# A spectral filter and a feed-forward block on one core: the steps of batch 0 reordered, one threshold moved to VectorE, all of batch 1's first DFT placed in the feed-forward stage

## The chip, the cores and the metric

The kernel runs on one core of a Trainium2 chip. The core has five engines that work side by side and wait for one another through semaphores: TensorE (PE in the profile, its weight loads PEld), VectorE (DVE), ScalarE (ACT), GpSimd (POOL) and SyncE (SP), which here issues every transfer. The metric is the device time of one execution in microseconds (us); lower is better.

## The reference

The input is x, 8 batches of 3008 positions with 256 features. What is computed, shortened:

```python
X = np.fft.rfft(x, axis=1)                       # along the 3008 positions
Yr = Xr @ w_r - Xi @ w_i + b_r
Yi = Xr @ w_i + Xi @ w_r + b_i
Y  = sign(Y) * max(abs(Y) - 0.01, 0)             # both parts, soft threshold
y  = np.fft.irfft(Y, n=3008, axis=1)
h  = y.reshape(24064, 256) @ w_in                # 256 -> 2048
out = (h - tanh(h)) @ w_out                      # 2048 -> 256
```

w_in and w_out are float64 in memory.

## The kernel before

The transform of 3008 = 47 x 64 positions is done in two stages of matmuls each way. `Forward` is the first stage (47 points): a chunk holds 4 of the 32 groups of a batch, and each chunk has two *parts* (split a tile into a high and a low fp32r half, L210; three matmuls, L217 to L219; copy out of PSUM, L233) and one store to the scratch tensor `a`. `Spectrum` is everything between the two inner stages for a pair of frequencies, 12 pairs in a batch: load `at`, second DFT stage (`transform`, L266), products with the linear layer (`cross`, L354, into the PSUM tiles ps_v and ps_t), threshold, inverse stage (L373) and a store of `zo` to the scratch tensor `z`. `Chunk` is the feed-forward block (FFN) for 5 of the 256 groups, 470 columns: load `zin` from `z`, last inverse stage (`time`, L403), then for each of 16 blocks f of 128 hidden features `up` (six matmuls into h, L416; tanh on ScalarE, L419; g = h - tanh on VectorE, L421; gh, a cast on ScalarE, L423; gl on VectorE, L425) and `down` (six matmuls into o, L437). One *slot* is one up and one down; up runs two slots ahead of down.

The program has two stages. The first (from L484) is written out by hand, and each engine works in the order of the code: batch 0's Forward, batch 0's Spectrum (`WholeSpectrum`, in plain fp32), conversion of part of the float64 weights, and the first two chunks' load and time. In it the loop of L537 runs over i = 0 to 12 and in one turn does the transform of pair i, the products of pair i-1, the threshold of pair i-2 and the inverse of pair i-3. In the loop of this stage a threshold is four adds on VectorE (L311, 64x256 each, tb from SBUF and ps_v from PSUM), two Relu activations on ScalarE (L363 `up`, L365 `mn`), and a subtraction on VectorE (L369 `mn`, the *join*). `sum` (L343) is a VectorE add that the products of the next turn need. The products of a pair need its sum, its copy xf (L338 on ScalarE) and a free ps_v buffer (there are two: that of the pair two before, free when that pair's four adds are done). `common` (L358) is the ScalarE copy tb that the four adds read.

A conversion of a *unit* of 128x512 weights from float64 is four closures (`split_f64`, L155): exponent, mantissa, scale, parts. Together they are four TENSOR_SCALAR (L161, L162, L165, L166) and two SCALAR_TENSOR_TENSOR (L172, L175) on VectorE, three operations on ScalarE (L167, L168, L176) and two on GpSimd (L169, L177). There are 16 units; the first stage before loads 6 of them, and works their closures off from the list `ops`.

The second stage is the FFN, from L599: `put(slot, ...)` files what is to run in which slot, and a scheduler orders each engine's instructions within the dependencies. The first 32 slots take chunks 0 and 1 by turns, f = 0 to 15. Ten units, six of batch 1's eight Forward chunks and batch 1's Spectrum are filed there.

## Time and profile before

| what | value |
|---|---|
| time, median of 3 runs (lowest to highest) | 2720.56 us (2716.45 to 2723.26) |
| time of the profiled execution | 2719.45 us |
| its span, first to last instruction | 2717.2 us |
| PE busy, share of the span | 2682.9 us, 99% |
| VectorE busy | 1746.0 us, 64% |
| ScalarE busy | 1388.9 us, 51% |
| GpSimd busy | 48.9 us, 2% |

The profiled execution's time is its span and 2.25 us around it. A row of the timeline gives start, length, engine, line, operation, what it writes and reads, how many instructions the row merges, and in brackets the idle time of the engine before it with what ended it. Matmul lengths overlap: the next one starts before the one before has ended, so from a row's start to the next row's start is its real price.

### The profile page before, as it was taken

The numbers are of one execution on the slowest core, as the hardware profiler recorded it, in microseconds if no ns is written. First come the engines' busy times: TensorE is split into PE (matmuls) and PEld (weight loads), VectorE is DVE, ScalarE is ACT, GpSimd is POOL, SyncE is SP. The second block draws the span as 40 slices with busy tenths as digits, with TensorE's granted clock in tenths as the row PEclk, the third lists the DMA queues.
The fourth block names the chain that finished last, engine by engine and source line by source line (L and its number), as shares of the span: only waits on it lengthen the run. The fifth ranks groups of instructions, "written<-read, shape, count | busy, mean of one in ns | idle before, by whom it ended". The sixth has DMA issues, their size and how long they took to land.

```text
span 2717.2 us, 36997 instructions
## 1 busy us (share of the span) xinstructions
PE 2682.9 (99%) x14159; PEld 2390.0 (88%) x14159; DVE 1746.0 (64%) x3056; ACT 1388.9 (51%) x2606; POOL 48.9 (2%) x39
## 2 busy tenths in 40 slices
PE   8889999999999999999999999999999999999999
PEld 6679888999889998899988999899988999998989
DVE  5796775766656666567665666656675667655555
ACT  5664455444554445545455454645446544444445
POOL 1230000000000000000000000000000000000000
PEclk9899999999999999999999999999999999999999
DMA  6442114111141113211023110311104111100000
GB/s 198 146 127 65 47 52 125 42 49 36 36 115 49 38 36 96 75 46 49 28 58 101 38 53 30 105 58 48 49 23 123 46 42 40 35 22 22 20 19 17
DMA packets 105137, 163.49 MB, mean 60 GB/s; under 512 B 7488, under 2 KB 70976, under 8 KB 104864
## 3 DMA queue, kind: packets, MB, share of 16 engines
q1 hardware_dynamic: 104960, 161.13, 19.6%
q8 instruction: 111, 1.82, 0.3%
q14 instruction: 66, 0.54, 0.1%
HBM read 86.13 MB, written 74.97 MB: 59 GB/s over the span
## 4 chain that ended last, share of the span: by engine, by line
PE 92%; DVE 5%; ACT 2%; issue 1%; DMA 1%; POOL 0%; SPq 0%; DVEq 0%; ACTq 0%
PE o L437 36%; PE h L416 36%; PE ps_v L286 4%; PE ps_i L403 4%; PE ps_f L266 3%; PE ps_t L286 2%; DVE y L311 1%; PE ps_f L217 1%; PE ps_f L219 1%; PE ps_f L218 1%; PE ps_i L322 1%; PE ps_i L323 1%; PE ps_i L321 1%; DVE g L421 1%; DVE gl L425 0%
## 5 line engine op out<-in xcount | busy, mean ns | idle before, releaser
L421 DVE TENSOR_TENSOR g<-h,th 128x470 f32<-128x470 f32 (+1 forms) x832 | 532.0, 639 | 554.6 <-ACT th L419 547.0
L419 ACT ACTIVATE th<-h 128x470 f32<-128x470 f32 (+1 forms) x832 | 464.1, 558 | 765.9 <-PE h L416 765.6
L425 DVE TENSOR_TENSOR gl<-g,gh 128x470 fp32r<-128x470 f32 (+1 forms) x832 | 534.5, 643 | 289.3 <-ACT gh L423 204.8
L423 ACT CAST gh<-g 128x470 fp32r<-128x470 f32 (+1 forms) x832 | 483.1, 581 | 392.6 <-DVE g L421 384.3
L437 PE MATMUL o<-gh,wout_l 128*128 128x470 f32 (+1 forms) x1664 | 632.8, 380 | 0.1
L437 PE MATMUL o<-gl,wout_h 128*128 128x470 f32 (+1 forms) x1664 | 617.1, 371 | 3.1 <-DVE gl L425 3.1
L437 PE MATMUL o<-gh,wout_h 128*128 128x470 f32 (+1 forms) x1664 | 616.1, 370 | 0.0
L416 PE MATMUL h<-yh,win_l 128*128 128x470 f32 (+1 forms) x1664 | 481.0, 370 | 4.1 <-DVE g L421 4.1
L416 PE MATMUL h<-yl,win_h 128*128 128x470 f32 (+1 forms) x1664 | 481.1, 370 | 1.6 <-DVE yl L408 1.5
L416 PE MATMUL h<-yh,win_h 128*128 128x470 f32 (+1 forms) x1664 | 480.1, 369 | 0.0
L437 PEld LDWEIGHTS o<-gl,wout_h 128*128 128x128 f32 x1664 | 313.1, 188 | 44.8 <-DVE gl L425 6.2
L416 PEld LDWEIGHTS h<-yh,win_l 128*128 128x128 f32 x1664 | 310.6, 188 | 41.9 <-DVE g L421 5.1
L437 PEld LDWEIGHTS o<-gh,wout_l 128*128 128x128 f32 x1664 | 313.4, 188 | 35.2 <-DVE ot L446 1.3
L416 PEld LDWEIGHTS h<-yl,win_h 128*128 128x128 f32 x1664 | 310.7, 188 | 37.7 <-DVE yl L408 2.2
L437 PEld LDWEIGHTS o<-gh,wout_h 128*128 128x128 f32 x1664 | 313.9, 189 | 32.2
L416 PEld LDWEIGHTS h<-yh,win_h 128*128 128x128 f32 x1664 | 310.7, 188 | 35.6
L311 DVE TENSOR_TENSOR y<-tb,ps_v 64x256 f32<-64x256 f32 x384 | 160.0, 417 | 9.7 <-ACT tb L358 5.7
L403 PEld LDWEIGHTS ps_i<-i,zin 96*128 96x128 f32 x1024 | 126.2, 192 | 3.0
L403 PE MATMUL ps_i<-i,zin 96*128 96x94 f32 x1024 | 127.7, 272 | 0.0
L91 DVE TENSOR_TENSOR x_l<-xt,x_h 94x512 fp32r<-94x512 f32 x128 | 87.8, 694 | 54.1 <-ACT x_h L90 54.1
L266 PEld LDWEIGHTS ps_f<-f,at 128*128 128x128 f32 x768 | 99.5, 189 | 9.3 <-issue 4.3
L266 PE MATMUL ps_f<-f,at 128*128 128x128 f32 x768 | 101.1, 273 | 1.8 <-DMA at<-a 1.8
(96 smaller groups left out, 2131.6 us busy)
## 6 DMA issues: line engine op xcount, KB each, us to landing
xt<-in_x SPq DMA_DIRECT2D x64, 384.0 KB, 3.6
at<-a SPq DMA_DIRECT2D x96, 256.0 KB, 2.8
z<-zo SPq DMA_DIRECT2D x96, 256.0 KB, 2.0
out<-ot SPq DMA_DIRECT2D x50, 470.0 KB, 3.0
a<-st SPq DMA_DIRECT2D x56, 384.0 KB, 3.2
zin<-z SPq DMA_DIRECT2D x44, 480.0 KB, 4.3
w_raw<-in_moe_w_in SPq DMA_DIRECT2D x8, 512.0 KB, 4.2
w_raw<-in_moe_w_out SPq DMA_DIRECT2D x8, 512.0 KB, 4.4
```

Of the source, the lines that this page charges most:

```text
L91: rest.tensor_tensor(out=lo, in0=src, in1=hi.bitcast(F32), op=ALU.subtract)
L217: nc.tensor.matmul(pv, f1h, xl, start=True, stop=False)
L266: nc.tensor.matmul(pv[:, t, jj], self.at[:, jj, t * P:(t + 1) * P], rhs, start=True, stop=True)
L286: nc.tensor.matmul(dst, lhs[:, t], rhs[:, t, :], start=n == 0, stop=n == 5)
L311: nc.vector.tensor_tensor(out=y[ri * 64:(ri + 1) * 64, jj, :], in0=common(jj, ri), in1=self.vv[jj * 64:(jj + 1) * 64, ri * D:(ri + 1) * D] ...
L403: nc.tensor.matmul(ps[:, k * 94:(k + 1) * 94], self.zt[:, k, t * P:(t + 1) * P], i2t[:, p * 94:(p + 1) * 94], start=True, stop=True,)
L416: nc.tensor.matmul(h[:, :n], lhs[:, t, f * P:(f + 1) * P], rhs[:, t, :n], start=k == 0, stop=k == 5)
L419: nc.scalar.activation(out=th[:, :n], in_=h[:, :n], func=AF.Tanh)
L421: nc.vector.tensor_tensor(out=g[:, :n], in0=h[:, :n], in1=th[:, :n], op=ALU.subtract)
L423: nc.scalar.copy(out=gh[:, :n], in_=g[:, :n])
L425: nc.vector.tensor_tensor(out=gl[:, :n], in0=g[:, :n], in1=gh[:, :n].bitcast(F32), op=ALU.subtract)
L437: nc.tensor.matmul(self.o[t][:, :n], lhs[:, f, t * P:(t + 1) * P], rhs[:, :n], start=f == 0 and k == 0, stop=f == NF - 1 and k == 2,)
```

## The change

Seven things change. (1) In the loop, `sum` of pair i and the products of pair i-1 stand ahead of the threshold of pair i-2; before, the four adds stood ahead of the sum. (2) The second Relu on ScalarE becomes a TENSOR_SCALAR on VectorE (add 0.01, then minimum with 0), and the join becomes an add. (3) Eight units are loaded and converted in the first stage, not six: two before the loop's second turn, two each in turns 2, 6 and 9; the closures come four each in turns 1 and 2 and two each in turns 4 to 11, where before they came two each in turns 2 to 9. (4) The three splits of the linear layer's matrices move from turns 3 to 5 to turns 0 to 2, and their low halves all to VectorE (two of them were on GpSimd). (5) The two Forward chunks of batch 1 that stood around the last two pairs leave the first stage; ten and fourteen idle matmuls stand in their place, where before twelve stood ahead of time. (6) In the FFN the eight units left start in slots 0, 3, 6, 10, 13, 15, 18 and 22, and all 16 parts of batch 1's Forward stand in slots 16 to 31 (before: 12 parts in slots 12 to 23). (7) Batch 1's 12 pairs start three slots apart from slot 40 (before: four apart from slot 31).

```diff
@@ -362,11 +362,11 @@
             up = self.temp("up", "th")
             nc.scalar.activation(out=up, in_=y, func=AF.Relu, bias=below)
             mn = self.mn = work.tile([P, 2, D], F32, name="mn", tag="tmp", bufs=4)
-            nc.scalar.activation(out=mn, in_=y, func=AF.Relu, bias=below, scale=-1.0)
+            nc.vector.tensor_scalar(out=mn, in0=y, scalar1=LAM, scalar2=0.0, op0=ALU.add, op1=ALU.min)
             self.up = up
 
         def join(self):
-            nc.vector.tensor_tensor(out=self.mn, in0=self.up, in1=self.mn, op=ALU.subtract)
+            nc.vector.tensor_tensor(out=self.mn, in0=self.up, in1=self.mn, op=ALU.add)
 
         def inverse(self):
             self.pz = ps_f.tile([P, 512], F32, name="ps_i1", tag="f")
@@ -517,92 +517,77 @@
         whole_lin, bias_rows = combine_linear(*lin_in, zero)
         i1h, i1l = split(i1f, "i1")
         units = [WholeSpectrum(0, jp) for jp in range(NJ // 2)]
-        for u in units[:3]:
-            u.load()
-        where = {0: "yh", 1: "yl", 2: "yh", 3: "yl", 7: "yh", 8: "yl"}
+        i2t = const.tile([96, NP * 94], F32, name="i2")
         raws, ops = [], []
-        i2t = const.tile([96, NP * 94], F32, name="i2")
         lin = []
-
-        def split_lin(k):
-            lin.append(split(whole_lin[k], f"w{k + 1}", rest=(nc.gpsimd, nc.vector, nc.gpsimd)[k]))
-
         NU = len(units)
-        LOOK = 2
-        following = [Forward(1, ch) for ch in range(LOOK)]
+        homes = [(work, "yh"), (work, "yl")] * 3 + [(load, "xt")] * 2
+        raw_at = {0: 2, 2: 2, 6: 2, 9: 2}
+        convert_at = (0, 4, 4, 0, 2, 2, 2, 2, 2, 2, 2, 2, 0)
+
+        def load_raw(n):
+            for _ in range(n):
+                k = len(raws)
+                raws.append(load_f64(k // 4, k % 4, *homes[k]))
+                if k % 2:
+                    ops.extend(convert([(m // 4, m % 4, raws[m]) for m in (k - 1, k)]))
+
+        def some(n):
+            for op in ops[:n]:
+                op()
+            del ops[:n]
 
         def unit(i):
             return units[i] if 0 <= i < NU else None
 
+        for u in units[:2]:
+            u.load()
         for i in range(NU + 1):
+            if i + 2 < NU:
+                units[i + 2].load()
+            load_raw(raw_at.get(i, 0))
             if unit(i - 2):
                 unit(i - 2).common()
             if unit(i):
                 unit(i).dft()
-            if unit(i - 2):
-                unit(i - 2).shrink()
-            if unit(i):
                 unit(i).sum()
             if unit(i - 1):
                 unit(i - 1).cross()
             if unit(i - 2):
+                unit(i - 2).shrink()
                 unit(i - 2).join()
             if unit(i - 3):
                 unit(i - 3).inverse()
                 unit(i - 3).put(unit(i - 3).pz)
-            if i + 3 < NU:
-                units[i + 3].load()
-            if i in where:
-                k = len(raws)
-                raws.append(load_f64(k // 4, k % 4, work, where[i]))
-                if k % 2:
-                    ops += convert([(n // 4, n % 4, raws[n]) for n in (k - 1, k)])
+            if i < 3:
+                lin.append(split(whole_lin[i], f"w{i + 1}"))
+            some(convert_at[i])
             if i in (4, 9):
                 sl = slice(0, 10 * 94) if i == 4 else slice(10 * 94, None)
                 nc.sync.dma_start(out=i2t[:, sl], in_=i2[:, sl])
-            if i in (5, 6):
-                following[i - 5].load()
-            if 3 <= i < 6:
-                split_lin(i - 3)
-            for op in ops[:(0, 0, 2, 2, 2, 2, 2, 2, 2, 2, 0, 0, 0)[i]]:
-                op()
-                ops.remove(op)
-        u9, u10, u11 = units[-3:]
-        for q in range(2):
-            following[0].split(q)
+        u10, u11 = units[-2:]
         u10.inverse()
+        u10.put(u10.pz)
         u11.common()
         u11.shrink()
-        for q in range(2):
-            following[0].dft(q)
-        u10.put(u10.pz)
         u11.join()
+        idle(10)
         u11.inverse()
         u11.put(u11.pz)
         for c in range(2):
             chunks[c].load()
-        for q in range(2):
-            following[0].keep(q)
-        for q in range(2):
-            following[1].split(q)
-        for op in ops[:6]:
-            op()
-        for q in range(2):
-            following[1].dft(q)
-            following[1].keep(q)
-        idle(12)
+        some(6)
+        idle(14)
         for c in range(2):
             for t in range(2):
                 chunks[c].time(t)
-            for op in ops[6 + c:7 + c]:
-                op()
-
-    for i in range(2):
-        put(2 * i - 2, ffn_weights, 1, 2 + i)
-    for i in range(8):
-        put(1 + 8 * i // 3, ffn_weights, 2 + i // 4, i % 4)
-    plan_forward(1, 8, 2, 3, LOOK)
-    plan_spectrum(1, 31, 4, 7, 2)
+            some(1)
+        some(9)
+
+    for i, slot in enumerate((0, 3, 6, 10, 13, 15, 18, 22)):
+        put(slot, ffn_weights, 2 + i // 4, i % 4)
+    plan_forward(1, 16, 2, 3)
+    plan_spectrum(1, 40, 3, 7, 2)
     for b in range(2, B):
         end = NF * (next(c for c in range(NCH) if begin[c] + sizes[c] > b * NP) - 1)
         plan_forward(b, end - 104, 2, 3)
```

The first place is VectorE in the loop, one turn. In the rows, y is the four adds, sf the sum, mn the threshold, w_s and w_m the weight conversion. Before:

```order
71 L311 TENSOR_TENSOR y<-tb_708,ps_v 64x256 x4
72 L343 TENSOR_TENSOR sf<-ps_f_710,xf 128x256
73 L369 TENSOR_TENSOR mn<-up,mn 128x512
74 L165 TENSOR_SCALAR w_m<-w_raw 128x512
75 L166 TENSOR_SCALAR w_s<-w_s 128x512
```

Now:

```order
71 L343 TENSOR_TENSOR sf<-ps_f_639,xf 128x256
72 L311 TENSOR_TENSOR y<-tb_637,ps_v 64x256 x4
73 L365 TENSOR_SCALAR mn<-y 128x512
74 L369 TENSOR_TENSOR mn<-up,mn 128x512
75 L165 TENSOR_SCALAR w_m<-w_raw 128x512
```

The sum, which needs the copy xf of the same turn, now stands ahead of the adds, and one VectorE instruction is new.

The second place is TensorE at the end of the first stage, the inverses of the last three pairs (L373). Before:

```order
123 L373 MATMUL ps_i_892<-mn,i_f 128x512
124 L373 MATMUL ps_i_905<-mn,i_f 128x512
125 L217 MATMUL ps_f_918<-x_0_0_l,f_h 96x512
...
130 L219 MATMUL ps_f_922<-x_0_1_h,f_l 96x512
131 L373 MATMUL ps_i_930<-mn,i_f 128x512
132 L217 MATMUL ps_f_967<-x_1_0_l,f_h 96x512
...
138 L493 MATMUL idle<-warm 128x512 x12
```

Now:

```order
123 L373 MATMUL ps_i_919<-mn,i_f 128x512
124 L373 MATMUL ps_i_924<-mn,i_f 128x512
125 L493 MATMUL idle<-warm 128x512 x10
126 L373 MATMUL ps_i_952<-mn,i_f 128x512
```

The twelve matmuls of batch 1's first four parts are gone from here; idle matmuls follow the last inverse as well, ahead of time.

The third place is VectorE at the start of the FFN, some slots in. Before:

```order
123 L421 TENSOR_TENSOR g<-h,th 128x470
124 L161 TENSOR_SCALAR w_s<-w_raw 128x512
125 L165 TENSOR_SCALAR w_m<-w_raw 128x512
126 L162 TENSOR_SCALAR w_s<-w_s 128x512
127 L421 TENSOR_TENSOR g<-h,th 128x470
128 L425 TENSOR_TENSOR gl<-g,gh 128x470
129 L166 TENSOR_SCALAR w_s<-w_s 128x512
130 L161 TENSOR_SCALAR w_s<-w_raw 128x512
131 L172 SCALAR_TENSOR_TENSOR w_s<-w_raw,w_s 128x512
132 L425 TENSOR_TENSOR gl<-g,gh 128x470
133 L175 SCALAR_TENSOR_TENSOR w_f<-w_f,w_s 128x512
```

Now, one of a pattern that repeats:

```order
145 L421 TENSOR_TENSOR g<-h,th 128x470
146 L175 SCALAR_TENSOR_TENSOR w_f<-w_f,w_s 128x512
147 L162 TENSOR_SCALAR w_s<-w_s 128x512
148 L425 TENSOR_TENSOR gl<-g,gh 128x470
149 L165 TENSOR_SCALAR w_m<-w_raw 128x512
150 L421 TENSOR_TENSOR g<-h,th 128x470
151 L166 TENSOR_SCALAR w_s<-w_s 128x512
152 L161 TENSOR_SCALAR w_s<-w_raw 128x512
153 L425 TENSOR_TENSOR gl<-g,gh 128x470
154 L172 SCALAR_TENSOR_TENSOR w_s<-w_raw,w_s 128x512
```

In both, the six VectorE instructions of a unit stand between two pairs of g and gl. In the order now, the last unit's last instruction (L175) stands behind 17 g and 16 gl; before, the last of the ten stood behind 20 of each and 7 splits of Forward parts. From batch 2's Forward on, the order of TensorE's last 11459 instructions of 13193 is the same in both.

## Rows read from the trace of the kernel before

**Rows 1.** Busy us by stretch: PE, PEld, DVE, ACT, POOL; clock (1.00: 2.4 GHz), DMA, GB/s.

```profile
104.00:116.00 12.00, 8.60 (x25) 5.50 (x26) 7.67 (x15) 6.32 (x13) 2.23 (x1) 0.61 0.54 159
200.00:250.00 50.00, 49.84 (x264) 44.63 (x263) 29.86 (x52) 24.67 (x46) 0.00 (x0) 1.00 0.26 81
```

**Rows 2.** Timeline, VectorE, the four adds of pairs 0, 4, 5, 10 and 11.

```profile
40.17 1.72 DVE L311 TENSOR_TENSOR y<-tb,ps_v 64x256 f32<-64x256 f32 x4 [2.58 <-ACT tb L358]
...
65.41 1.71 DVE L311 TENSOR_TENSOR y<-tb,ps_v 64x256 f32<-64x256 f32 x4 [0.96 <-ACT tb L358]
...
71.31 1.72 DVE L311 TENSOR_TENSOR y<-tb,ps_v 64x256 f32<-64x256 f32 x4 [0.63 <-ACT tb L358]
...
95.23 1.71 DVE L311 TENSOR_TENSOR y<-tb,ps_v 64x256 f32<-64x256 f32 x4
...
100.66 1.72 DVE L311 TENSOR_TENSOR y<-tb,ps_v 64x256 f32<-64x256 f32 x4
```

**Rows 3.** Timeline, ScalarE and VectorE around the adds of pair 4.

```profile
65.01 0.36 ACT L358 COPY tb<-ps_t 128x256 f32<-128x256 f32 x1
65.28 0.59 ACT L338 COPY xf<-ps_f 128x512 f32<-128x512 f32 x1
...
67.16 0.42 DVE L343 TENSOR_TENSOR sf<-ps_f,xf 128x256 f32<-128x256 f32 x1
...
67.79 0.71 ACT L365 ACTIVATE mn<-y,below 128x512 f32<-128x512 f32 x1
...
68.53 0.69 DVE L369 TENSOR_TENSOR mn<-up,mn 128x512 f32<-128x512 f32 x1 [0.95 <-ACT mn L365]
...
69.93 0.42 DVE L165 TENSOR_SCALAR w_m<-w_raw 128x512 uint32<-128x512 uint32 x1
```

**Rows 4.** Timeline from the last inverse to the FFN; landing of the zin loads.

```profile
104.52 2.08 PE L373 MATMUL ps_i<-mn,i_f 128*128 128x512 f32 x2 [2.75 <-DVE mn L369]
...
109.28 0.87 SPq L393 DMA_DIRECT2D zin<-z  x2
...
115.54 4.60 PE L403 MATMUL ps_i<-i,zin 96*128 96x94 f32 x40
119.92 0.67 PE L416 MATMUL h<-yh,win_l 128*128 128x470 f32 x2
...
DMA to landing us min/median/max: 4.2/5.1/6.1
```

**Rows 5.** Timeline, GpSimd and VectorE, in the loop of the first stage.

```profile
50.22 1.39 POOL L91 TENSOR_TENSOR w_l<-wr_f,w_h 128x512 fp32r<-128x512 f32 x1 [3.12 <-ACT w_h L90]
...
50.40 1.50 DVE L161 TENSOR_SCALAR w_s<-w_raw 128x512 uint32<-128x512 uint32 x1
...
71.15 1.28 POOL L169 TENSOR_TENSOR w_f<-w_f,w_m 128x512 f32<-128x512 f32 x1 [4.34 <-ACT w_m L168]
```

**Rows 6.** Timeline, TensorE, in the FFN.

```profile
190.86 0.69 PE L416 MATMUL h<-yh,win_l 128*128 128x470 f32 x2 [1.48 <-DVE g L421]
...
194.21 0.58 PE L416 MATMUL h<-yh,win_l 128*128 128x470 f32 x2
...
195.47 0.40 PE L217 MATMUL ps_f<-x_l,f_h 94*96 94x512 f32 x1
...
196.17 0.38 PE L437 MATMUL o<-gh,wout_l 128*128 128x470 f32 x1
```

**Rows 7.** Groups of instructions, VectorE, 131 to 193 us: busy, mean, idle before.

```profile
L425 DVE TENSOR_TENSOR gl<-g,gh 128x470 fp32r<-128x470 f32 x18 | 13.5, 757 | 0.0
L421 DVE TENSOR_TENSOR g<-h,th 128x470 f32<-128x470 f32 x17 | 10.8, 635 | 0.0
...
L175 DVE SCALAR_TENSOR_TENSOR w_f<-w_f,w_s 128x512 f32<-128x512 f32 x9 | 6.1, 681 | 0.6 <-POOL w_f L169 0.6
...
L91 DVE TENSOR_TENSOR x_l<-xt,x_h 94x512 fp32r<-94x512 f32 x7 | 5.8, 834 | 0.0
```

**Rows 8.** Who waited for whom, 200 to 400 us: total, times, longest.

```profile
PE ps_v L286 <- DVE xl L278: 0.5, 3, 0.2
```

## The prediction

> **What bounds the kernel now.** The page of the profile says PE 99%, so I first asked where that holds. The windows view gives it: from 200 to 250 us PE is busy 49.84 of 50 us at granted clock 1.00 [rows 1]. There an instruction more or less on VectorE or ScalarE changes nothing, a matmul more or less counts in full, and from batch 2's Forward on TensorE's order is unchanged. So the change decides itself before 200 us, and by what it moves into the part behind. Before 200 us I read three stretches.
>
> The loop of the first stage is a circuit through three engines. In the timeline the adds of pair 4 end at 65.41 + 1.71 = 67.12, the second Relu starts on ScalarE at 67.79, the join on VectorE at 68.53, 1.41 us after the adds; the conversions come behind it, and then the next adds wait for tb [rows 2, 3]. One turn with two closures took 71.31 − 65.41 = 5.90 us, the last one, with two splits of batch 1's Forward, 100.66 − 95.23 = 5.43 [rows 2].
>
> The tail is one chain: join, inverse at 104.52 (2.08 us, after 2.75 us of waiting), zin issued at 109.28, time at 115.54, first up at 119.92 [rows 4]. The granted clock over 104 to 116 us is 0.61, so between the levels of 1.2 and 2.4 GHz [rows 1]; the inverse at 2.08 I read as one at 1.2, its price at 2.4 being half, 1.04.
>
> At the start of the FFN VectorE sets the pace: the groups from 131 to 193 us show it idle for 0.6 us in all [rows 7], and PE waiting 1.48 us for a g as late as 190.86 [rows 6]. An up or a down costs PE 195.47 − 194.21 = 1.26 us and a part of Forward 196.17 − 195.47 = 0.70 [rows 6]. From 119.92 to 190.86 PE did 21 ups, 19 downs and 7 parts (counted in the order): 40 x 1.26 + 7 x 0.70 = 55.3 us of work in 70.9. It lost 15.6.
>
> **The change, part by part.** *Circuit.* With the negative part on VectorE the join no longer waits for ScalarE: the new instruction starts at the end of the adds, the join some 0.77 behind it (the TENSOR_SCALAR on a tile of that size takes 0.42 [rows 3], and about 0.35 for reading up, my estimate from the first Relu's 0.71, which the join still needs). That gains 1.41 − 0.77 = 0.64 a turn. Against it, the sum now stands ahead of the adds on VectorE and needs xf of the same turn. Before, the adds followed tb after 65.41 − 65.01 = 0.40; now tb, xf (0.59) and the sum (0.42, some 0.08 of it overlapped) come first [rows 3], which is about 0.85 later. Net +0.2 in a turn where tb is set by the join's followers, 0 where it is set by the products, which now start sooner. Over the nine turns from pair 1's to pair 10's adds I take half, +0.9 (0 to 1.8).
>
> *Conversions and splits in the loop.* Turns 1 and 2 take eight closures where two stood, and three splits. A closure costs VectorE about 0.76: a unit is four at 0.42 [rows 3] and two at 0.68 [rows 7], in four closures. Six more are 4.6 us, three splits at 0.68 are 2.0, and 2.6 of that falls into the idle time ahead of pair 0's adds [rows 2]: +4.0 (3.0 to 4.6). In turns 3 to 5 the splits go (about −1.9, three at 0.6 or so), and one more turn has closures (+1.7, a turn's 5.90 against some 4.2 that the adds, the join and the copies leave): −0.2.
>
> *End of the loop.* The last turn now goes join, inverse, zo, tb, adds on engines in order: 1.45 + 2.08 + 0.59 + 0.36 + 1.72 = 6.2, against 5.43: +0.8 (zo is a ScalarE copy of xf's shape and goes by its 0.59). Here I take the inverse at the lower clock, since PE has nothing for about 3 us ahead of it, as it had 2.75 ahead of the 2.08 [rows 4]. Then the join gains 0.6, and the last inverse 1.0, if the ten idle matmuls bring the clock up: it starts at about 109.3 us instead of 104.52. Sum at the zin issue: +0.9 + 4.0 − 0.2 + 0.8 − 0.6 − 1.0 = **+3.9**.
>
> *Tail.* Issue to time took 6.26 us before, since the twelve idle matmuls stood in the way (time's row names no wait), and the load's median landing is 5.1 [rows 4]: −1.2. Time took 4.38 [rows 4] at a clock that was coming up; now PE idles longer between the fourteen idle matmuls and time, so 5.2, nearer its own row than twice that: +0.8. So the FFN starts **+3.5** later, at 123.4. With adds and landing at their low ends it starts +0.9 later (or at 119.9, rival C), with landing at 6.1 and time wholly at the lower clock +9.
>
> *Start of the FFN.* Two units and seven splits less stand among the first g and gl. The unit's price there follows from the groups: (62.0 − 0.6 − 13.5 − 10.8 − 5.8) / 9 = 3.5 us [rows 7]. Now the last unit ends behind 17 g and 16 gl: 17 x 0.635 + 16 x 0.757 + 8 x 3.5 = 50.9 us, and 3.7 for the first up, its tanh and the wait for yl. That is 54.6 us in which PE does 18 ups and 16 downs, 34 x 1.26 = 42.8. It loses 11.8 instead of 15.6: **−3.8**.
>
> *Behind it.* Four more parts of Forward stand where PE has no gap: 4 x 0.70 = **+2.8**. Batch 1's pairs three slots apart load VectorE more; in the stretch of pairs four apart PE waited for it three times, 0.2 at most [rows 8]. Between 0 and 12 x 0.2 I take **+0.5**. The matmuls of the eight parts that left the first stage's tail cost nothing there, since they lay in waits of the chain.
>
> Sum: 3.5 − 3.8 + 2.8 + 0.5 = +3.0. From the profiled execution's 2719.45, which is 1.1 under the median, that is 2722.5; I predict **2723**, with 2715 to 2731 as this case's own range.
>
> *A rule weighed at the new instruction.* A TENSOR_SCALAR of this shape took 1.50 us at 50.40, beginning 0.18 after a GpSimd operation of 1.39, against the usual 0.42; adds at 71.31, which read PSUM, took their usual 1.72 beside a GpSimd operation from 71.15 on [rows 2, 3, 5]. So the four adds don't suffer, but the new instruction and the join can, 1.1 us a time. I price that at nothing: the GpSimd operation of 71.15 began 4.0 us after the adds' end at 67.12 and lasts 1.3, which leaves it done before the next adds are, some 6 us after.
> The Trainium skill, "SBUF — State Buffer", section "Who interferes with whom", says why: a VectorE instruction with two SBUF inputs, or a tensor_scalar in a two-port mode, and a GpSimd instruction that reads SBUF take one port pair as an exclusive lock, and the second waits in full. The rows named agree; by this rule the sum would be unchanged if they miss each other, and rival B's if they meet.
>
> **Rivals.** *A, the jam at the start of the FFN dissolves.* If fewer GpSimd operations fall on VectorE's instructions, a unit costs 4 x 0.42 + 2 x 0.68 = 3.0 and a gl 0.64: 33 x 0.635 + 8 x 3.0 = 45 us, 5.7 less. Time 2717. For it: no splits between; against: all eight units keep their GpSimd operations. Only with the FFN start at its low end too does it pass 2712.
> *B, slower: the lock in the loop.* The threshold and join stand on the circuit in each of 12 turns. If a GpSimd operation (two for each of six units) still runs as the adds end, each costs 1.1 [rows 5]: +13, 2736. It decides from the point at which a GpSimd operation begins less than 1.3 us ahead of the adds' end; against it, the margin of about 0.7 to 1.5 us worked out above.
> *C, nothing arrives late.* The four closures of turns 1 and 2 may be hidden as the first turns wait for products anyway, and the shorter join pays for the sum: FFN start at 119.9, sum −0.5, 2719.
>
> **How the numbers follow.** What a measurement of this kernel tells from no change is about 0.3%, 8.2 us. Chances: forecast 0.6, A 0.15, B 0.1, C 0.15. Slower takes B and the forecast's upper end (time at the lower clock, a late landing), 0.1 + 0.08; faster A and C at their low ends and what the forecast has below 2712, 0.08; the rest, 0.74, is within. The range of 2714 to 2732 holds all but B and the outer tenth of the others.
>
> **What would show it.** Right: the join less than 0.9 us behind the adds, adds of pair 11 near 106 to 108 us, first up at 121 to 126, VectorE without idle time until some 55 us later, PE full from there. Wrong: adds, thresholds or joins of 1.1 us more than their usual beside GpSimd (B), a unit of 3.0 on VectorE (A), the first up at 120 (C), or PE gaps behind 200 us, which I price at 0.5 in all.

## The result, and the profile after

Over nine runs of each the changed kernel took 2727.06 us (2723.66 to 2733.53) against 2719.72 us (2715.32 to 2723.26) of the kernel before: ratio 1.003, 95% interval 1.002 to 1.0041. That is 7.3 us more, less than the 8.2 us that the prediction called no change, though its interval lies clear of 1; it is inside the range of 2714 to 2732, and more than the +3.0 worked out. The profiled execution took 2723.66 us, the shortest of the nine and 3.4 under their median, with a span of 2721.5.

The milestones of both profiled executions, in us from the span's start, beside what the prediction's steps give for the difference:

| milestone | before | after | difference | forecast |
|---|---|---|---|---|
| first second-stage DFT of batch 0 starts | 34.49 | 32.04 | −2.45 | 0 |
| adds of pair 1 end | 47.79 | 52.57 | +4.8 | +4.0 |
| adds of pair 10 end | 96.94 | 101.18 | +4.2 | +4.7 |
| adds of pair 11 end | 102.38 | 106.73 | +4.35 | +5.5 |
| zin issued | 109.28 | 112.28 | +3.0 | +3.9 |
| time starts | 115.54 | 117.69 | +2.15 | +2.7 |
| first up starts (time lasts) | 119.92 (4.38) | 125.98 (8.29) | +6.06 | +3.5 |
| first up to end of span | 2597.3 | 2595.5 | −1.8 | −0.5 |

Two things in it were not foreseen. Time took 8.29 us, not 5.2. And the changed kernel's profiled execution had come to its first second-stage DFT 2.45 us earlier, in a part that the change doesn't touch; measured from that DFT, pair 11's adds end at 67.9 us before and at 74.7 now, so the loop lost 6.8 us. From that DFT to the first up it is 85.4 us before and 93.9 now: with equal starts the first up would come 8.5 us later and the span would grow by 8.5 − 1.8 = 6.7, near the 7.3 of the medians. In the profiles of all versions below that DFT starts anywhere from 32.04 to 34.78. That is why one profile's time must not be set against another's to the microsecond, and why each verdict below goes by medians and each reason by a stretch of the trace.

The DFT's rows, timeline of TensorE, first the kernel before (with the adds of pair 1 on VectorE), then the changed one:

```profile
34.49 2.02 PE L266 MATMUL ps_f<-f,at 128*128 128x128 f32 x16 [1.78 <-DMA at<-a]
...
46.07 1.72 DVE L311 TENSOR_TENSOR y<-tb,ps_v 64x256 f32<-64x256 f32 x4 [0.62 <-ACT tb L358]
```

```profile
32.04 3.24 PE L266 MATMUL ps_f<-f,at 128*128 128x128 f32 x16 [1.94 <-DMA at<-a]
```

The tail of the changed kernel, timeline of TensorE and of SyncE's DMA queue:

```profile
108.27 1.12 PE L373 MATMUL ps_i<-mn,i_f 128*128 128x512 f32 x2 [0.36 <-DVE mn L369]
108.83 3.76 PE L493 MATMUL idle<-warm 128*128 128x512 f32 x14
...
112.28 0.86 SPq L393 DMA_DIRECT2D zin<-z  x2
...
117.69 8.59 PE L403 MATMUL ps_i<-i,zin 96*128 96x94 f32 x40 [5.10 <-issue]
125.98 1.13 PE L416 MATMUL h<-yh,win_l 128*128 128x470 f32 x2
```

The last inverse took 1.12 us where it took 2.08 before [rows 4]: the ten idle matmuls ahead of it did what they were forecast to do. Ahead of time TensorE had nothing for 5.10 us, and the 40 matmuls took nearly twice their 4.6 us. The windows view says the same of the clock (the column behind the five engines); the stretches are 104 to 116, 116 to 131, 200 to 250 and 250 to 400 us:

```profile
104.00:116.00 12.00, 8.23 (x27) 5.49 (x25) 10.01 (x18) 5.50 (x10) 2.86 (x2) 0.86 0.43 124
116.00:131.00 15.00, 13.26 (x57) 12.36 (x58) 5.98 (x11) 5.53 (x11) 1.28 (x2) 0.66 0.54 150
...
200.00:250.00 50.00, 50.00 (x245) 43.33 (x244) 27.95 (x45) 29.75 (x55) 0.00 (x0) 1.00 0.46 132
250.00:400.00 150.00, 149.93 (x862) 136.51 (x861) 115.91 (x213) 77.69 (x149) 0.00 (x0) 1.00 0.16 50
```

From 104 to 116 us the clock is better than before (0.86 against 0.61 [rows 1]), from 116 on it is near its lower level (1.2 of 2.4 GHz is 0.5). Behind 200 us TensorE is full, with 0.07 us of gaps in 200: pairs three slots apart bring no wait.

In the loop, timeline of ScalarE, VectorE and TensorE from the closures of turn 2 to the next products:

```profile
46.73 2.36 DVE L175 SCALAR_TENSOR_TENSOR w_f<-w_f,w_s 128x512 f32<-128x512 f32 x2
...
48.52 1.22 ACT L176 CAST win_h<-w_f 128x512 fp32r<-128x512 f32 x2 [2.11 <-DVE w_f L175]
...
49.65 0.36 ACT L358 COPY tb<-ps_t 128x256 f32<-128x256 f32 x1
...
50.53 0.42 DVE L343 TENSOR_TENSOR sf<-ps_f,xf 128x256 f32<-128x256 f32 x1 [1.44 <-ACT xf L338]
...
50.87 1.70 DVE L311 TENSOR_TENSOR y<-tb,ps_v 64x256 f32<-64x256 f32 x4
...
52.73 0.47 PE L348 MATMUL ps_v<-brow,ones 33*128 33x512 f32 x1 [3.95 <-DVE y L311]
53.12 2.50 PE L354 MATMUL ps_v<-w_f,xf 128*128 128x256 f32 x5
```

The four closures of turn 2 end with two L175 on VectorE and the casts L176 on ScalarE. ScalarE works in order, so tb and xf of the next turn stand behind casts that wait 2.11 us for L175, and VectorE then stands idle for 1.44 us until xf is there. The prediction charged these closures with VectorE's time alone. The next products then start after 3.95 us without work, and five of them take 2.50 us; in the turns before, eight took 1.99.

The lock (rival B) did not reach the threshold: all twelve new instructions took 0.43 us and all twelve joins 0.69, the last ones here:

```profile
106.83 0.43 DVE L365 TENSOR_SCALAR mn<-y 128x512 f32<-128x512 f32 x1
107.52 0.69 DVE L369 TENSOR_TENSOR mn<-up,mn 128x512 f32<-128x512 f32 x1 [0.26 <-ACT up L363]
```

In one turn it passed narrowly: a GpSimd operation (L177) ended at 101.12 us, the adds of pair 10 at 101.18; in the others GpSimd was done 0.9 us or more before. At another place of the loop a meeting did happen: at 39.42 us L161, ahead of pair 0's sum on VectorE, began beside a GpSimd operation of 1.46 us and took 1.50 in place of 0.42.

The FFN's start, timeline of VectorE and GpSimd, one unit of eight:

```profile
148.64 1.59 POOL L169 TENSOR_TENSOR w_f<-w_f,w_m 128x512 f32<-128x512 f32 x1 [1.08 <-ACT w_m L168]
...
149.06 1.68 DVE L425 TENSOR_TENSOR gl<-g,gh 128x470 fp32r<-128x470 f32 x1
...
153.23 1.30 POOL L177 TENSOR_TENSOR wout_l<-w_f,wout_h 128x512 fp32r<-128x512 f32 x1 [3.00 <-ACT wout_h L176]
...
153.31 1.50 DVE L165 TENSOR_SCALAR w_m<-w_raw 128x512 uint32<-128x512 uint32 x1
```

Both GpSimd operations of the unit meet a VectorE instruction: gl takes 1.68 instead of 0.64, L165 1.50 instead of 0.42. The groups of VectorE from 131 to 185 us tell how often:

```profile
L425 DVE TENSOR_TENSOR gl<-g,gh 128x470 fp32r<-128x470 f32 x17 | 16.9, 1000 | 0.0
...
L165 DVE TENSOR_SCALAR w_m<-w_raw 128x512 uint32<-128x512 uint32 x8 | 8.7, 1093 | 0.0
```

16.9 − 17 x 0.64 = 6.0 us on gl and 8.7 − 8 x 0.42 = 5.3 on L165, at 1.04 and 1.08 a meeting: five or six units of the eight are hit in both places.

What the start of the FFN costs can be counted as the prediction counted it, at 1.26 us for an up or a down and 0.70 for a part. From the first up to the 31st TensorE does 30 ups, 28 downs and 12 parts in both kernels, 81.5 us of work. It took 97.33 us before and 96.43 now, so it lost 15.8 and 14.9. From the 31st to the 101st up it took 249.61 us before and 249.08 now, although four more parts stand there now. Timeline of TensorE at the 31st and the 101st up, first before, then now:

```profile
217.25 0.58 PE L416 MATMUL h<-yh,win_l 128*128 128x470 f32 x2
...
466.86 0.58 PE L416 MATMUL h<-yh,win_l 128*128 128x470 f32 x2
```

```profile
222.41 0.58 PE L416 MATMUL h<-yh,win_l 128*128 128x470 f32 x2
...
471.49 0.58 PE L416 MATMUL h<-yh,win_l 128*128 128x470 f32 x2
```

### The profile page after: what moved, and what is told of

It is laid out like the page before. It is cut to its first block, busy times and chain, and to the rows that moved or that the text cites. A ratio compares the mean times of both kernels' runs of the same rounds, so it can differ in the third digit from the quotient of the medians.

```text
span 2721.5 us, 37028 instructions
## 1 busy us (share of the span) xinstructions
PE 2688.2 (99%) x14171; PEld 2397.0 (88%) x14171; DVE 1753.4 (64%) x3070; ACT 1382.8 (51%) x2594; POOL 47.0 (2%) x37
## 3 DMA queue, kind: packets, MB, share of 16 engines
q8 instruction: 111, 1.82, 0.3%
## 4 chain that ended last, share of the span: by engine, by line
PE 94%; DVE 4%; ACT 1%; DMA 1%; issue 1%; POOL 0%; SPq 0%; DVEq 0%; ACTq 0%; POOLq 0%
PE o L437 37%; PE h L416 37%; PE ps_v L286 4%; PE ps_i L403 4%; PE ps_f L266 3%; PE ps_t L286 2%; PE ps_f L217 1%; PE ps_f L219 1%; PE ps_f L218 1%; DVE y L311 1%; PE ps_i L322 1%; PE ps_i L323 1%; PE ps_i L321 1%; DVE gl L425 1%; DVE g L421 0%
```

## The experiments

All versions with their milestones. Each median stands beside that of the kernel before in the same comparison; "loop" is from the start of the first second-stage DFT to the end of pair 11's adds, "FFN" from the first up to the end of the span, "lost" what TensorE loses from its first up to its 31st by the count above (with 8 parts in version 8), all in the profiled execution.

| version | median | before | ratio, 95% interval | loop | time | FFN | lost |
|---|---|---|---|---|---|---|---|
| kernel before (profile) | – | – | – | 67.9 | 4.38 | 2597.3 | 15.8 |
| changed kernel | 2727.06 | 2719.72 | 1.003, 1.002 to 1.0041 | 74.7 | 8.29 | 2595.5 | 14.9 |
| 1 before, reordered | 2721.64 | 2719.31 | 1.0008, 0.9999 to 1.0017 | 69.7 | 4.39 | 2598.1 | 16.5 |
| 2 changed, old order | 2728.61 | 2719.31 | 1.0036, 1.0023 to 1.0049 | 76.1 | 8.52 | 2597.5 | 16.5 |
| 3 changed, 36 idle | 2722.00 | 2719.31 | 1.0013, 1.0004 to 1.0022 | 77.3 | 4.52 | 2595.2 | 13.9 |
| 4 changed, slow closures | 2717.36 | 2719.31 | 0.9995, 0.9986 to 1.0003 | 72.9 | 8.52 | 2594.2 | 13.7 |
| 5 slow closures, 32 idle | 2716.03 | 2719.37 | 0.9988, 0.9979 to 0.9997 | 72.6 | 4.38 | 2594.1 | 13.3 |
| 6 the same, 24 idle in front | 2715.51 | 2719.37 | 0.9985, 0.9976 to 0.9994 | 70.6 | 4.38 | 2594.4 | 13.4 |
| 7 changed, no GpSimd add in the FFN | 2717.00 | 2719.37 | 0.9994, 0.9985 to 1.0003 | 75.6 | 8.53 | 2589.0 | 8.4 |
| 8 version 5, six units, two chunks | 2718.63 | 2719.37 | 1.0000, 0.9991 to 1.0009 | 68.8 | 4.38 | 2591.9 | 14.3 |
| 9 version 6, FFN's add on VectorE | 2706.62 | 2721.01 | 0.9950, 0.9937 to 0.9962 | 70.6 | 4.38 | 2585.4 | 5.0 |
| 10 version 6, all adds on VectorE | 2710.59 | 2721.01 | 0.9964, 0.9951 to 0.9978 | 69.4 | 4.39 | 2589.7 | 9.0 |
| 11 before, FFN's add on VectorE | 2716.23 | 2719.41 | 0.9985, 0.9976 to 0.9994 | 71.1 | 4.39 | 2592.6 | 11.7 |

The same loop code takes 67.9 us in the kernel before and 71.1 in version 11, and 74.7, 77.3 and 75.6 us in the changed kernel and versions 3 and 7. So a difference of up to 3 us between the loops of two profiles shows nothing by itself.

**1 and 2, the reorder alone and undone.** The edit of 1 is the first two hunks of the change and this order in the loop; 2 takes the same out of the changed kernel.

```diff
             if unit(i):
                 unit(i).dft()
-            if unit(i - 2):
-                unit(i - 2).shrink()
-            if unit(i):
                 unit(i).sum()
             if unit(i - 1):
                 unit(i - 1).cross()
             if unit(i - 2):
+                unit(i - 2).shrink()
                 unit(i - 2).join()
```

> The kernel before with parts 1 and 2 of the change alone: sum and products ahead of the threshold, the second Relu on VectorE, the join an add. Theory of the prediction (the sum now behind xf gives back what the earlier join gains, some 0.1 a turn): the adds of pair 11 end 0.5 to 2 us later after the first second-stage DFT than the 67.9 us of the kernel before, and the time is 0 to 2 us over the kernel before. Rival (the reorder is what makes the whole change slower): 4 to 8 us over it, with the adds of a turn without conversions 4.5 us or more apart. Third (the reorder is a gain that the other parts hide): 3 us or more under it.

> The changed kernel with parts 1 and 2 undone: the four adds ahead of the sum, the second Relu on ScalarE, the join a subtraction; all the rest as changed. Theory (the reorder is nearly free, the loss is in turns 1 and 2 and in time's clock): 0 to 2 us under the changed kernel. Rival (the reorder is the loss): 4 to 8 us under it. Third (the reorder pays): over it by 2 us or more.

Alone it cost 2.3 us by the medians, a little over the theory's 2, with an interval that still holds no change, and 1.8 us in the loop. The nine turns from pair 1 to pair 10 took 49.4 us against 49.2 before, so the gain and the loss inside a turn do cancel there; the 1.8 us stand ahead of them, as pair 1's adds end 15.1 us behind the DFT's start in place of 13.3, with the DFT at 2.02 us in both. Undone in the changed kernel it made that 1.5 us slower by the medians and 2.0 by their differences to before, from two comparisons whose intervals overlap. Its loop of 76.1 us lies among those of the changed kernel and versions 3 and 7. The last two turns took 12.8 us with the old order and 10.9 to 11.9 in those three. So the reorder is not the loss, which would have shown as 4 to 8 us; whether it pays in the changed kernel these runs do not tell.

**3, more idle matmuls ahead of time.**

```diff
-        idle(14)
+        idle(36)
```

> The changed kernel with 36 idle matmuls ahead of time in place of 14, so that TensorE works until the zin loads land. Theory (time took 8.3 us because the clock had fallen in the 5.1 us without work ahead of it): time takes 4.4 to 5 us, the granted clock from 116 to 131 us is over 0.9 in place of 0.66, the first up starts some 3.5 us earlier after time's start is known, and the kernel is 3 to 4.5 us under the changed kernel. Rival (time is slow for another reason, as a weight load or the loads' landing): no change, or later by what the idle matmuls overrun, 0 to 3 us over it.

The windows view of this version from 116 to 131 us, and TensorE's timeline at time and, for later, at the products of the loop's turn 3:

```profile
116.00:131.00 15.00, 14.33 (x84) 12.22 (x82) 10.24 (x15) 7.51 (x14) 4.24 (x4) 1.00 0.82 208
```

```profile
55.76 2.77 PE L354 MATMUL ps_v<-w_f,xf 128*128 128x256 f32 x6
58.31 1.91 PE L354 MATMUL ps_t<-wr_f,sf 128*128 128x256 f32 x4
...
121.48 4.73 PE L403 MATMUL ps_i<-i,zin 96*128 96x94 f32 x40
```

Time took 4.52 us at clock 1.00, and the median is 5.1 under that of the changed kernel (from two comparisons; 4.7 by their differences to before), a little more than the theory's 3 to 4.5. The last inverse stands 9.42 us ahead of time in both versions, so the added idle matmuls ended just as the loads landed. The clock was the cause: in all profiles of the table time takes 4.4 to 4.5 us where TensorE works right up to it, and 8.3 to 8.5 where it had stood idle for 4.1 to 5.6 us. The other rows show it once more where nothing was edited: behind the gap of turn 2 the products of ps_t took 1.91 us here and 1.03 elsewhere, and pair 3's adds start 7.9 us behind pair 2's, in the profile of the changed kernel 6.4. The same program pays for the same gap more in some executions than in others.

**4, the closures at the old pace.**

```diff
-        convert_at = (0, 4, 4, 0, 2, 2, 2, 2, 2, 2, 2, 2, 0)
+        convert_at = (0, 0, 2, 2, 2, 2, 2, 2, 2, 2, 2, 2, 0)
```

> The changed kernel with the closures of the conversions no longer four each in turns 1 and 2: none in turn 1, two in each of turns 2 to 11, so that 12 in place of 8 are left for the tail. Theory (the closures of turns 1 and 2 hold tb and xf on ScalarE behind casts that wait for VectorE and GpSimd): the adds of pair 1 end 13 to 16 us after the first second-stage DFT starts, in place of 20.5, those of pair 11 3 to 5 us earlier, and as the four closures have room in the wait for zin, the kernel is 2.5 to 5 us under the changed kernel. Rival (the tail has no room, and the closures come back ahead of the first yl): 0 to 2 us under, or over.

Timeline of this version, ScalarE and VectorE in the turn that ends with pair 1's adds, and TensorE at the first second-stage DFT and at time:

```profile
32.46 3.39 PE L266 MATMUL ps_f<-f,at 128*128 128x128 f32 x16 [1.97 <-DMA at<-a]
...
46.66 0.37 ACT L358 COPY tb<-ps_t 128x256 f32<-128x256 f32 x1
46.92 0.59 ACT L338 COPY xf<-ps_f 128x512 f32<-128x512 f32 x1
...
47.88 1.70 DVE L311 TENSOR_TENSOR y<-tb,ps_v 64x256 f32<-64x256 f32 x4
...
115.32 8.82 PE L403 MATMUL ps_i<-i,zin 96*128 96x94 f32 x40 [4.10 <-ACT w_m L168]
```

The median fell by 9.7 us (9.3 by the differences to before), more than forecast, to where no difference from the kernel before shows. Its profile shows less than that: pair 1's adds end 17.1 us behind the DFT's start (20.5 in the changed kernel, 20.7 and 20.8 in versions 3 and 7 with the same loop; 13 to 16 expected), pair 11's 1.8 us earlier (3 to 5 expected), the FFN 1.3 shorter. These sizes were missed. The four closures did have room in the tail. The profiled executions are 3.5 us apart where the medians are 9.7, since that of the changed kernel lies 3.4 us under its median and this one 2.8 over. What makes the executions of one kernel differ by so much is shown only in part, by version 3's rows at the lower clock.

**5 and 6, both corrections, and the clock in front.** 5 has 4's closures and `idle(32)` ahead of time; 6 has besides:

```diff
-        idle(16)
+        idle(24)
         whole_lin, bias_rows = combine_linear(*lin_in, zero)
```

> The changed kernel with both corrections together: closures two a turn from turn 2, and 32 idle matmuls ahead of time in place of 14. Theory (two separate causes, the clock in time and the closures in front of tb): the gains add up, time takes 4.4 to 5 us, and the kernel is 3 to 5 us under the version with slow closures alone, at 2712 to 2715. Rival (both act through the same wait for zin): no gain over the better of the two, 2716 to 2719.

> The version before it in this list with 24 idle matmuls in place of 16 between batch 0's Forward and its first second-stage DFT. In the profile of the changed kernel that DFT's 16 matmuls took 3.2 us behind 1.94 us without work, in that of the kernel before 2.0 us behind 1.78. Theory (the same clock effect as at time): the 16 matmuls take 2.0 us, the first products start 1 to 1.5 us earlier after the DFT's start, and the kernel is 1 to 1.5 us under the version before it. Rival (the idle matmuls run into the moment at which the loads of at land, or the clock comes up anyhow): no difference, or up to 1 us over.

The gains did not add up in the medians: 5 is 1.4 us under 4, by their differences to before, where time alone gave back 4.1. Each of the two intervals reaches 2.3 us or more to either side, so the medians neither show the 4.1 nor exclude it. The rival's number came out, though its reason (both through the wait for zin) isn't shown by these traces: its profile has time at 4.38 and the first up at 118.89, 4.95 earlier than 4's. For 6 the DFT did come at full clock:

```profile
33.44 2.02 PE L266 MATMUL ps_f<-f,at 128*128 128x128 f32 x16 [1.22 <-DMA at<-a]
```

The loop became 2.0 us shorter (70.6, and 70.6 again in version 9, whose loop is the same), the median only 0.5, within its uncertainty.

**7, GpSimd's add left out in the FFN.** The add L169 of the eight units converted in the FFN is gone, so their weights lack the upper mantissa.

> The changed kernel without the GpSimd add (L169) of the eight units that the FFN converts, so that these weights are left without their upper mantissa part and GpSimd has one operation a unit there in place of two. Theory of the prediction (VectorE sets the pace at the start of the FFN and loses about 1.1 us each time it meets a GpSimd operation): a unit costs VectorE 3.0 to 3.2 us in place of 3.5, VectorE stays without idle time, the last of the eight units ends 3 to 5 us sooner after the first up, and the kernel is 3 to 5 us under the changed kernel. Rival (the lock is hidden behind ScalarE's turn, the pace is set by the chain tanh, g, gh, gl): no difference, with idle time on VectorE.

VectorE's groups from 131 to 185 us (lines one further on: L426 is gl, L165 the first mantissa step, L173 the scale):

```profile
L426 DVE TENSOR_TENSOR gl<-g,gh 128x470 fp32r<-128x470 f32 x19 | 13.4, 711 | 0.7 <-ACT gh L424 0.7
L422 DVE TENSOR_TENSOR g<-h,th 128x470 f32<-128x470 f32 x19 | 12.1, 637 | 2.0 <-ACT th L420 2.0
L165 DVE TENSOR_SCALAR w_m<-w_raw 128x512 uint32<-128x512 uint32 x8 | 7.7, 959 | 0.0
L173 DVE SCALAR_TENSOR_TENSOR w_s<-w_raw,w_s 128x512 uint32<-128x512 uint32 x8 | 5.5, 682 | 0.0
```

The FFN is 6.5 us shorter than the changed kernel's, all of it at the start (8.4 us lost in place of 14.9), and by the differences to before the kernel is 9.7 us under the changed one, beyond the 3 to 5 expected; the two profiled executions are 4.0 apart. The last unit's L175 ends 51.4 us behind the first up in place of 58.7. The mean gl fell from 1.00 to 0.71 us, while L165, which meets the GpSimd operation that stayed, is still at 0.96. A unit itself, by the prediction's subtraction, costs 3.1 us in both kernels, and VectorE was not without idle time: it waits 2.7 us for ScalarE here. The rival falls all the same: GpSimd's meetings with VectorE and the wait of L175 for the add, which this run doesn't separate, set the pace.

**8, back to six units and two chunks.** Of the first stage's loads the two at turn 9 are gone, ten units go to the FFN, and two Forward chunks of batch 1 stand in the tail, around 12 and 8 idle matmuls.

> The version with slow closures and 32 idle matmuls, but with parts 3, 5 and 6 of the change undone in size: six units in the first stage, ten in the FFN, two of batch 1's Forward chunks back in the tail between 12 and 8 idle matmuls, twelve parts in the FFN. Theory (the two units less in the FFN gain 3.8 us, the four parts more cost 2.8): 0 to 2 us over the version with slow closures and 32 idle matmuls. Rival one (the parts weigh more than the units): 2 us or more under it. Rival two (the units are the gain): 3 us or more over it.

Timeline of TensorE in its tail:

```profile
115.99 0.74 PE L217 MATMUL ps_f<-x_l,f_h 94*96 94x512 f32 x1 [5.63 <-DVE x_l L91]
...
118.67 2.89 PE L493 MATMUL idle<-warm 128*128 128x512 f32 x8
```

It is 2.6 us over version 5, a little beyond the theory's 2. The sum hides two opposite terms: the FFN is 2.2 us shorter, rival one's direction, since the four parts weigh 2.8 there and the two units little; but from the DFT's start to the first up it takes 4.2 us longer, as the second chunk's matmuls wait 5.63 us for splits that stand behind closures on ScalarE and VectorE. Between these two versions the two units cost the FFN 0.6 us (2.8 less 2.2) and not 3.8. One reason is in the trace: behind the first up stand 11 L175 here and 10 in version 5, so that only one unit more ends there.

**9, 10 and 11, the add moved to VectorE.** In 9 for the FFN's units (`one`), in 10 for all, in 11 for the FFN's ten units of the kernel before. Nothing is left out.

```diff
+            if one:
+                nc.vector.scalar_tensor_tensor(out=w, in0=low, scalar=2.0**-32, in1=m, op0=ALU.mult, op1=ALU.add)
+            else:
                 nc.scalar.mul(out=w, in_=low, mul=2.0**-32)
                 nc.scalar.copy(out=m.bitcast(F32), in_=m)
                 nc.gpsimd.tensor_tensor(out=w, in0=w, in1=m.bitcast(F32), op=ALU.add)
```

> The version with slow closures, 32 idle matmuls ahead of time and 24 ahead of the first second-stage DFT, and in the eight units that the FFN converts one SCALAR_TENSOR_TENSOR on VectorE (low half times 2^-32 plus mantissa) in place of two ScalarE operations and the GpSimd add. Nothing is left out. Theory (the meetings with GpSimd cost VectorE more than the add itself would): a unit has 0.68 us more of its own and one GpSimd operation in place of two, the FFN from first up to end is 2 to 5 us shorter than the 2594.4 us of that version, and the kernel is 2 to 4 us under it. Rival (VectorE is the bound by its own work, and 8 x 0.68 = 5.4 us more of it costs what the lock gave): within 1.5 us of it, or up to 3 us over.

> The same in all sixteen units, so in the loop of the first stage too. Theory (in the loop a closure delays the turn by its wait from VectorE over ScalarE and GpSimd back to VectorE, and by its ScalarE operations ahead of tb): the turns with closures are 0.3 to 0.8 us shorter, the adds of pair 11 end 2 to 5 us earlier after the first second-stage DFT, and the kernel is 1 to 4 us under the version with the FFN's units alone. Rival (VectorE's own work sets the turn): the turns with a mantissa closure are 0.6 us longer, and the kernel is 1 to 3 us over it.

> The kernel before with the mantissa add of the ten units that its FFN converts on VectorE, as in the version that did so with the eight. It tells whether the plan of the change (eight units in the FFN, sixteen parts) pays once the meetings with GpSimd are fewer. Theory (the meetings were most of the 15.6 us that TensorE lost there): the FFN from first up to end is 6 to 11 us shorter than the 2597.3 us of before, and the kernel is 6 to 11 us under before. Rival (ten units with the add are VectorE's own work, 10 x 3.7 + 41 x 0.63 + 7 x 0.68 = 68 us against 55 us of TensorE's, so the loss stays): 0 to 3 us under before.

The windows view from 131 to 185 us, of version 6 and of version 9:

```profile
131.00:185.00 54.00, 48.92 (x214) 38.15 (x212) 51.01 (x83) 31.97 (x60) 23.02 (x16) 1.00 0.29 84
```

```profile
131.00:185.00 54.00, 53.27 (x251) 46.07 (x250) 53.51 (x98) 30.00 (x57) 16.28 (x8) 1.00 0.36 113
```

and of version 11:

```profile
131.00:185.00 54.00, 49.95 (x225) 41.01 (x225) 54.00 (x97) 29.39 (x55) 16.32 (x8) 1.00 0.34 100
```

Version 9 is 10.5 us under version 6 by their differences to before (2 to 4 expected), and 14.4 under the kernel before, the best of all. Its FFN is 9.0 us shorter, with 5.0 us lost at the start in place of 13.4. TensorE is busy 53.27 of 54 us there, 48.92 in version 6, with VectorE at 53.51: both are nearly full. VectorE's own work went up by 8 x 0.68 = 5.4 us, and still TensorE waits less for it. The edit also takes two ScalarE operations from each unit; what part of the gain is theirs no run separates. One meeting of the GpSimd operation that stayed (L180 here is L177 before; L428 is gl, L168 the new add):

```profile
154.30 2.54 POOL L180 TENSOR_TENSOR wout_l<-w_f,wout_h 128x512 fp32r<-128x512 f32 x1 [5.16 <-ACT wout_h L179]
...
155.05 0.64 DVE L428 TENSOR_TENSOR gl<-g,gh 128x470 fp32r<-128x470 f32 x1
...
156.17 1.22 DVE L168 SCALAR_TENSOR_TENSOR w_f<-w_raw,w_m 128x512 f32<-128x512 uint32 x1
```

Here it is GpSimd that takes 2.54 instead of 1.30, where nobody waits for it, and VectorE loses 0.54. Over the window GpSimd's eight operations took 16.28 us, where 8 x 1.30 would be 10.4.

Version 10 shortens the loop by 1.2 us more, less than expected, and is 4 us slower as a whole. Its rival had the direction, but neither the size (1 to 3 us over) nor the reason, since the loop as a whole did not get longer. The place is the FFN's start, where 9.0 us are lost in place of 5.0: eight VectorE steps of closures stand between the last yl and the first g, four in version 9. TensorE's timeline and the window of 126 to 131 us:

```profile
124.11 0.70 PE L414 MATMUL h<-yh,win_l 128*128 128x470 f32 x2 [3.21 <-DVE g L419]
```

```profile
126.00:131.00 5.00, 4.47 (x11) 3.62 (x12) 4.58 (x8) 2.95 (x6) 1.25 (x1) 0.50 0.00 0
```

3.21 us without work, and the clock at 0.50 behind it. Version 11 took 3.2 us from the kernel before, hardly more than its rival's 0 to 3: its FFN became 4.7 us shorter, not 6 to 11, with VectorE at 54.00 of 54 us and TensorE at 49.95. Its last unit ends 72.4 us behind the first up, of which the rival worked out 68 as VectorE's own work. So with ten units VectorE's own work still binds in the main, and the change's plan of the FFN pays 7.2 us there (2592.6 against 2585.4) once the meetings are fewer, 6.7 of it at the start (11.7 against 5.0 lost).

## Why the prediction came out as it did

The verdict held: no change that stands clear of 0.3%, on the slower side. The sum held less well than its result: two steps, conversions and time, cost some 3 us more than worked out, and two others, the start of the FFN and what stands behind it, missed by 2.9 and 3.8 us in opposite directions, which is luck. The steps one by one:

- **What bounds.** Right that TensorE is full behind 200 us: the gaps with pairs three slots apart are 0.07 us in 200. Wrong that little but the four parts would move there, see the last step but one.
- **Circuit.** Right for the nine turns that it counts: +0.2 (version 1) where +0.9 (0 to 1.8) was forecast. The turns ahead of pair 1's adds had no term, and there version 1 lost 1.8. The join starts 0.79 us behind the adds (107.52 against 106.73), worked out as 0.77.
- **Conversions in turns 1 and 2.** The mechanism was too narrow. The term "+4.0 (3.0 to 4.6)" counted closures on VectorE. What also holds the turn is ScalarE's order: casts behind L175 behind GpSimd's add, ahead of tb and xf. Pair 1's adds end 20.5 us behind the DFT's start, 13.3 before: 7.2 in place of 4.0. Of it, 3.4 goes with six of the eight closures (20.5 to 17.1 in version 4) and 1.2 is the DFT itself at the lower clock; the other 2.6 are not separated, with the reorder (1.8 in version 1) and the splits in it. The earlier start of that execution covered 2.45 of the 7.2.
- **End of the loop.** +0.1 from pair 10's adds to pair 11's (5.43 before, 5.55 now) in place of +0.8, since the inverse of pair 10 ran in 1.10 us and not 2.08; in version 3 the same inverse took 2.05. I had the right two numbers, and which one holds changes from execution to execution.
- **Time.** The step that failed most plainly. "now PE idles longer between the fourteen idle matmuls and time, so 5.2, nearer its own row than twice that": it was 8.29, close to twice. The upper end of the range had it ("time wholly at the lower clock"). Version 3 shows that the clock was the cause. It made the step +3.9 instead of +0.8. Measured from the DFT's start the first up comes 8.5 us later, where +3.5 was forecast: 3.1 of the 5.0 between them are time's, and 1.9 the steps ahead of it, whose excess the early start of that execution hides in the table.
- **Start of the FFN, four parts and pairs.** The sum −0.5 stands near the −1.8 measured, but by luck. The start gained 0.9 us (15.8 lost before, 14.9 now; 13.9 in version 3, whose first ups come at the full clock) in place of 3.8. From the 31st to the 101st up TensorE took 0.5 less, although four parts at 0.70 were added: the rest became 3.3 us shorter, where +0.5 was taken. Gaps of TensorE that are gone make 0.9 of it; the cause of the other 2.4 is open. What the start's term had wrong is the meetings and the waits: it kept gl at its old mean of 0.757, and now that GpSimd's add meets gl, 17 of them took 1.00 each, 4 us more; VectorE idled 1.9 us, mostly for that add; and the first ups ran at the lower clock. A unit by itself was cheaper, 3.1 and not 3.5. The last one ended 58.7 us behind the first up and not 54.6. That the meetings and the waits for GpSimd make most of the loss is shown by versions 7 and 9 (8.4 and 5.0 lost). Rival A asked for them to vanish by themselves; they did not. (In A's own sum 50.9 less 45 is 5.9, not 5.7.)
- **Rival B** did not come about, for the reason given: no GpSimd operation ran as the adds ended. The margin of "0.7 to 1.5 us" was 0.6 in the one turn that the prediction had worked out (71.15 + 1.28 to 71.31 + 1.72), and 0.06 in the narrowest turn of the changed kernel. **Rival C** missed, the closures were not hidden.

The rule of the Trainium skill, "SBUF — State Buffer", section "Who interferes with whom", agrees with these rows: gl has two SBUF inputs, L165 is a TENSOR_SCALAR (whether in a two-port mode no view tells), both wait for a GpSimd operation that reads SBUF, and in version 9 GpSimd waits for VectorE. What I did not draw from it is that the loser can change: with the add on VectorE a good part of the price of the meetings fell on GpSimd, whose operations took 2.04 us in the mean in place of 1.30.

What stays open: how the loop and its clock differ from one execution of a kernel to the next, since each has one profile only; what made the FFN from the 31st up on 2.4 us shorter; and whether the gains of versions 3 and 4 add up in 5.

## What to carry to other kernels

Where a step is moved, follow the in-order engines beside the one that does its work: here two casts on ScalarE that waited 2.11 us for VectorE stood ahead of a copy that the next turn needed, and with six closures out of those two turns pair 1's adds ended 3.4 us earlier. Fill the gaps of TensorE ahead of a serial step with idle matmuls up to the moment at which its data land, and read the granted clock of the stretch to see whether it worked. Where VectorE is full and GpSimd helps it, look for instructions far over their usual length beside GpSimd's (1.68 in place of 0.64 us here); giving VectorE the work itself can make it faster.

## What was unexpected of the hardware

An add that VectorE did itself in 0.68 us replaced one on GpSimd that took 1.3 to 1.6 us beside it, and the FFN became 9.0 us shorter over eight units, more than 1 us each. The granted clock after a gap was not the same each time: the DFT's 16 matmuls took 3.20 us behind 1.82 us without work (version 5) and 3.24 behind 1.94, but 2.02 us behind 1.78 or 2.01, the inverse of pair 10 took 1.10 or 2.05 behind 2.87 us. Behind 5.10 us it stayed near 1.2 GHz through the whole 8.3 us of time and the first ups.
